# Projecting q and k by channels and placing them with on-chip DMAs, in a gated mix of segmented attention and a one-token FFN

## The chip, the cores and the metric

The kernel runs on one core of a Trainium2 chip. The metric is the device time of one execution in microseconds. The core has TensorE (PE; its weight loads are listed as PEld), VectorE (DVE), ScalarE (ACT) and GpSimd (POOL). SyncE (SP) computes nothing here; it issues all the DMAs, one after the other, in one queue.

## The reference

The input x has 2048 tokens of 640 channels. Branch A is attention with 32 heads of 20 channels over 4 segments of 512 tokens, each causal by itself, plus a memory that earlier segments have written. Branch B sends the one token with the highest router score through an FFN. A gate per token mixes the two.

```python
q, k, v = heads(x @ wq), heads(x @ wk), heads(x @ wv)
phi = lambda t: where(t > 0, t + 1, exp(t))
M = z = 0
for s in range(4):
    p = softmax(qs @ ks.T * scale + causal_mask)
    a_mem = phi(qs) @ M / (phi(qs) @ z + 1e-6)
    o = g * a_mem + (1 - g) * (p @ vs)        # g = sigmoid(beta), per head
    M, z = M + phi(ks).T @ vs, z + sum(phi(ks))
a = concat(o) @ wo
r = x @ w_r;  i = argmax(r)
b = x;  b[i] += sigmoid(r[i]) * (silu(x[i] @ w_gate) * (x[i] @ w_up)) @ w_down
out = sigmoid(x @ gate_w) * a + (1 - sigmoid(x @ gate_w)) * b
```

## The kernel before

**Units.** The heads are taken in four quarters (`hq`) of eight. A unit `u` is one quarter in one segment, 16 units in all. A group `n` is four heads of a unit, 32 groups in all.

**Projection (L249 to L284).** A chunk `q` is 128 tokens of a unit, 64 chunks. `load_x` brings the chunk of the transposed x, `split_x` makes a rounded high part (ScalarE) and a low part (GpSimd). 15 matmuls (5 slices of channels, 3 products of high and low parts) give `acc`, 128 tokens x 480 columns of q, k and v for eight heads. In the first quarter two more columns carry the router score and the gate. `evac` (L157) puts high, low and high again of q and k side by side in `qkn`, so that one matmul over 60 rows gives a logit of full accuracy, puts v into `va`, and phi of q and k into `phi`.

**Turning q and k (L179).** The logits need channels on the partitions. `stacks` transposes `qkn` on TensorE, four transposes for q and four for k in each chunk, and ScalarE copies the result into `qs` and `ks`, of which there are three each, one per unit.

**Memory (L189, L208, L220).** `memory_read` transposes phi of q, multiplies it with the memory `mbd`, and keeps the result in `nums`; `memory_norm` divides and gates. `memory_write` multiplies phi of k with v, one small matmul for each head and chunk, and adds into the diagonal blocks of `mbd`.

**Attention.** `a_step` computes logits for a pair of heads, queries on the partitions, and VectorE takes their maxima under the mask. `m_split` and `m_rows` (L310, L316) turn the negative maxima into two extra rows of `qs`: four transposes for each pair of heads, then a copy of two partitions by ScalarE and one by VectorE. `b_step` (L324) computes the logits again, keys on the partitions and the maxima already subtracted by those rows; ScalarE takes the exponential and GpSimd masks the diagonal. `pv_step` multiplies with v. `norm` (L368) transposes, divides, adds the memory part and, except in the last quarter, stores to `otok` in DRAM.

**Output.** `out_proj` transposes 128 rows of the attention's output, multiplies with wo in 30 matmuls of 320 columns, mixes in branch B and stores. The FFN's matmuls are spread over the middle of the run.

**Order.** TensorE's order is written out by hand: the loop at L622 goes through 34 groups of six slots. A slot has a `b_step` of group n and an `a_step` of the next group or the one after, and between them `fill` runs as much projection as the line `chunks[0] >= (at + 9) / 3 + 4.5` asks for, about 7.5 chunks ahead. The order on the other engines and on SP is made by a scheduler when the program is built; each executes it in order. PSUM has one buffer for `a`, one for `b`, one for `pv` and three of tag `misc` for everything else.

Of the kernel before, what the change touches and what calls it, by code (L numbers as in the profile page):

```python
# [7 lines left out]
F32 = mybir.dt.float32  # L8
# [10 lines left out]
KT = D // 128  # L19
NQ = 4  # L20
HQ = H // NQ
WQ = 3 * HQ * DH
FF = 1728
VW = DH + 1
ST = 2 + 3 * DH
SCALE = DH ** -0.5
NEG = -1e30

# [6 lines left out]
def tile_infini_mod(  # L35
# [51 lines left out]
    NB = 3  # L87
    qkn, qs, ks, va = [], [], [], []
    for i in range(2):
        t = one.tile([128, 2, HQ, 64], F32R, name=f"qkn{i}")  # L90
        nc.vector.memset(t[:, 0, :, :2].bitcast(F32), 0.0)
        nc.vector.memset(t[:, 1, :, :2].bitcast(F32), 1.0)
        nc.vector.memset(t[:, :, :, ST:].bitcast(F32), 0.0)
        qkn.append(t)
    for i in range(NB):
        qs.append(one.tile([128, HQ // 2, L], F32R, name=f"qs{i}"))
        ks.append(one.tile([128, HQ // 2, L], F32R, name=f"ks{i}"))
        t = one.tile([128, 4, HQ * VW + 11], F32, name=f"va{i}")
        nc.vector.memset(t, 1.0)
        va.append(t)  # L100
    phi = []
    for i in range(5):
        t = one.tile([128, 2, HQ, 32], F32, name=f"phi{i}")
        nc.gpsimd.memset(t, 0.0)
        phi.append(t)
    mneg = one.tile([128, 4, 2, 66], F32R, name="mneg")
    nc.gpsimd.memset(f32(mneg), 0.0)
    mbd = one.tile([128, 2, 128], F32, name="mbd")
    nc.gpsimd.memset(mbd, 0.0)
    rg = one.tile([128, 2, S // 128], F32, name="rg")  # L110

# [3 lines left out]


    W, wraw = {}, {}

    def load_w(key, k):
        if key[0] == "o":  # L120
            src = wo[128 * k:128 * k + 128, 320 * key[1]:320 * key[1] + 320]
        else:
            c0 = WQ * key[1] + (2 if key[1] else 0)
            src = wc[128 * k:128 * k + 128, c0:c0 + WQ + (0 if key[1] else 2)]
        t = pool.tile([128, WQ + 2], F32, tag="wraw", bufs=2, name="wraw")
        nc.sync.dma_start(t[:, :src.shape[1]], src)
        wraw[key, k] = t[:, :src.shape[1]]

    def split_w(key, k):
        raw = wraw.pop((key, k))  # L130
        n = raw.shape[1]
        hi = pool.tile([128, WQ + 2], F32R, tag="whi", bufs=2 * KT, name="whi")[:, :n]
        lo = pool.tile([128, WQ + 2], F32R, tag="wlo", bufs=2 * KT, name="wlo")[:, :n]
        split(hi, lo, raw, nc.vector)
        W[key, k] = hi, lo


    xraw, xhi, xlo = {}, {}, {}

    def load_x(q):  # L140
        t = pool.tile([128, KT, 128], F32, tag="xraw", bufs=2, name="xraw")
        s0 = (q % 16) * 128
        nc.sync.dma_start(t, xT[:, s0:s0 + 128].rearrange("(k p) t -> p k t", p=128))
        xraw[q] = t

    def split_x(q):
        xhi[q] = pool.tile([128, KT, 128], F32R, tag="xhi", bufs=2, name="xhi")
        xlo[q] = pool.tile([128, KT, 128], F32R, tag="xlo", bufs=2, name="xlo")
        split(xhi[q], xlo[q], xraw.pop(q), nc.gpsimd)
# [3 lines left out]
    done_units = [0]  # L153
    oldest = [0]
    chunks = [0.0]

    def evac(q, acc):  # L157
        u, c = divmod(q, 4)
        hq, s = divmod(u, SEG)
        t = qkn[q % 2]  # L160
        n = HQ * DH
        src = acc[:, :2 * n].rearrange("p (a h d) -> p a h d", a=2, d=DH)
        hi = sub(t, 2, [[HQ * 64, 2], [64, HQ], [1, DH]])
        nc.scalar.copy(hi, src)
        lo = sub(t, 2 + 2 * DH, [[HQ * 64 - DH, 2], [64, HQ], [1, DH]])
        nc.vector.tensor_tensor(out=lo, in0=src, in1=f32(hi), op=OP.subtract)
        hi2 = sub(t, 2 + DH, [[HQ * 64 + DH, 2], [64, HQ], [1, DH]])
        nc.vector.tensor_copy(hi2, f32(hi))
        v = sub(va[u % NB], c * (HQ * VW + 11), [[VW, HQ], [1, DH]])
        nc.scalar.copy(v, acc[:, 2 * n:3 * n].rearrange("p (h d) -> p h d", d=DH))  # L170
        a0, a1 = (0 if s > 0 else 1), (2 if s < SEG - 1 else 1)
        e = phi[q % 5][:, a0:a1, :, :DH]
        nc.scalar.activation(e, src[:, a0:a1], AF.Relu, scale=-1.0)
        nc.scalar.activation(e, e, AF.Exp, scale=-1.0)
        nc.vector.scalar_tensor_tensor(out=e, in0=src[:, a0:a1], scalar=1.0, in1=e, op0=OP.add, op1=OP.max)  # L175
        if hq == 0:
            nc.vector.tensor_copy(rg[:, :, 4 * s + c], acc[:, 3 * n:3 * n + 2])

    def stacks(q):  # L179
        u, c = divmod(q, 4)  # L180
        t = qkn[q % 2]
        for a, dst in ((0, qs), (1, ks)):
            tp = psum.tile([128, 4, 128], F32R, tag="misc", bufs=3, name="tp")
            for p in range(4):
                nc.tensor.transpose(tp[:, p, :], t[:, a, 2 * p:2 * p + 2, :].rearrange("p h r -> p (h r)"), identr)  # L185
            yield 4 * 56
            nc.scalar.copy(dst[u % NB][:, :, 128 * c:128 * c + 128], f32(tp))  # L187

    def memory_read(q):  # L189
        u, c = divmod(q, 4)  # L190
        tp = psum.tile([128, 2, 128], F32, tag="misc", bufs=3, name="tp")
        for g in range(2):
            nc.tensor.transpose(tp[:, g, :], phi[q % 5][:, 0, 4 * g:4 * g + 4, :].rearrange("p h r -> p (h r)"), identf)
        pt = pool.tile([128, 2, 128], F32, tag="pt", bufs=2, name="pt")
        nc.scalar.copy(pt, tp)
        yield 220
        nm = psum.tile([128, 2, 4, VW], F32, tag="misc", bufs=3, name="nm")
        for g in range(2):
            nc.tensor.matmul(nm[:, g], pt[:, g, :], mbd[:, g, :].rearrange("p (j r) -> p j r", r=32)[:, :, :VW],
                             start=True, stop=True)  # L200
        yield 430
        if c == 0:
            nums[u] = pool.tile([128, 4, HQ * VW], F32, tag="num", bufs=3, name="num")
        nc.scalar.copy(nums[u][:, c, :], nm.rearrange("p g j e -> p (g j e)"))
        if c == 3:
            memory_norm(u)

    def memory_norm(u):  # L208
        hq = u // SEG
        nu = nums.pop(u).rearrange("p c (h e) -> p c h e", e=VW)  # L210
        rm = pool.tile([128, 4, HQ], F32, tag="rm", bufs=2, name="rm")
        nc.vector.tensor_scalar(rm, nu[:, :, :, DH], 1e-6, None, op0=OP.add)
        nc.vector.reciprocal(rm, rm)
        gt = sub(gate, HQ * hq, [[0, 4], [1, HQ]])
        nc.vector.tensor_tensor(out=rm, in0=rm, in1=gt, op=OP.mult)
        rb = sub(rm, 0, [[HQ, 4], [1, HQ], [0, DH]])
        om[u] = nu[:, :, :, :DH]
        nc.gpsimd.tensor_tensor(out=om[u], in0=om[u], in1=rb, op=OP.mult)

    def memory_write(u):  # L220
        s = u % SEG
        mp = psum.tile([128, 2, 32], F32, tag="misc", bufs=3, name="mp")
        for g in range(2):
# [6 lines left out]
        for j in range(4):  # L230
            dst = mbd[32 * j:32 * j + 32, :, 32 * j:32 * j + VW]
            src = mp[32 * j:32 * j + 32, :, :VW]
            if s == 0:
                nc.vector.tensor_copy(dst, src)
            else:
                nc.vector.tensor_tensor(out=dst, in0=src, in1=dst, op=OP.add)

    def post(q):
        u, c = divmod(q, 4)
        s = u % SEG  # L240
        yield from stacks(q)
        if s > 0:
            yield from memory_read(q)
        if c == 3:
            if s < SEG - 1:
                yield from memory_write(u)
            done_units[0] = u + 1

    def projections():  # L249
        NCH = 4 * NQ * SEG  # L250
        for q in range(NCH):
            u, c = divmod(q, 4)
            hq, s = divmod(u, SEG)
            assert u < oldest[0] + NB
            if q + 2 < NCH:
                load_x(q + 2)
            if s == 2 and hq + 1 < NQ:
                key = ("q", hq + 1)
                if c == 0:
                    load_w(key, 0)  # L260
                load_w(key, c + 1)
                split_w(key, c)
# [451 lines left out]
```

## Time and profile before

| | |
|---|---|
| median of 3 runs | 866.21 us (865.5 to 866.72) |
| profiled execution, its own time | 871.42 us |
| span of the profiled execution | 869.7 us |
| mean granted TensorE clock | 0.929 |
| DVE busy | 539.0 us (62%) |
| ACT busy | 479.9 us (55%) |
| POOL busy | 236.0 us (27%) |
| DMA | 62.15 MB, 23.2% of 16 engines' time |

The span runs from the first to the last instruction. In a row of groups stand the source line, the engine, the operation, what it writes and reads, the shapes and the count; then busy time and mean duration, then the engine's idle time ahead of it with what ended that. In a timeline the columns are start, duration, engine, line and operation, and in brackets an idle time before it. The row of the granted clock gives it in tenths of full speed for 40 equal slices of the span. Rows of DMA issues give minimum, median and maximum of the time that the issuing instruction takes on SP, in ns.

### The profile page before, as it was taken

The page shows a single profiled execution, that of the slowest core. Times are in us where ns is not written, and L with a number is a line of the kernel's source. Part 1 is how long each engine was busy: PE and PEld are TensorE (multiplying, and loading weights), DVE is VectorE, ACT ScalarE, POOL GpSimd, SP SyncE. Part 2 cuts the span into 40 slices and gives each one's busy share as a digit, 9 for nine tenths or more (in the row PEclk, how much of TensorE's full clock was granted, in tenths as well). Part 3 has the DMA queues.
Part 4 walks back from the last instruction along what each step waited for, and adds up shares of the span by engine and source line. Part 5 has one row for each costly group of instructions (what it writes and reads, how often), then busy time and mean ns, then how long its engine had stood idle before and what let it go on. Part 6 is the DMA issues. An engine that isn't in the chain of part 4 may idle for free. (4 is left out here: it accounts for less than half of the span.)

```text
span 869.7 us, 15435 instructions
## 1 busy us (share of the span) xinstructions
PE 757.4 (87%) x5664; PEld 492.6 (57%) x5664; DVE 539.0 (62%) x1764; ACT 479.9 (55%) x915; POOL 236.0 (27%) x307
## 2 busy tenths in 40 slices
PE   5769898968898989989987979889998989999998
PEld 2646454634565555645554555545565545676787
DVE  5365665856666665767575665767666747575354
ACT  4536564735566655646564664656665747344422
POOL 3212322323333232233243232324232322111100
PEclk9989898979898998999998998989998989899999
DMA  6311011231101023524222232401010111133353
GB/s 183 116 30 32 16 44 34 77 58 26 52 26 52 16 61 98 176 82 136 81 57 76 72 102 67 137 23 52 27 48 29 32 32 39 47 105 107 122 164 124
DMA packets 68027, 62.15 MB, mean 71 GB/s; under 512 B 4262, under 2 KB 59312, under 8 KB 67952
## 3 DMA queue, kind: packets, MB, share of 16 engines
q1 hardware_dynamic: 67952, 61.17, 23.2%
q8 instruction: 45, 0.74, 0.4%
q14 instruction: 30, 0.25, 0.1%
HBM read 50.66 MB, written 9.19 MB: 69 GB/s over the span
## 5 line engine op out<-in xcount | busy, mean ns | idle before, releaser
L306 DVE CUSTOM_DVE_ANT_0 junk<-a,mask 128x512 bf16<-128x512 f32 (+3 forms) x512 | 248.8, 486 | 119.8 <-PE a L303 111.6
L336 ACT ACTIVATE p<-bt 128x768 f32<-128x768 f32 (+1 forms) x192 | 169.5, 883 | 162.2 <-PE bt L332 161.2
L339 POOL TENSOR_SCALAR_AFFINE_SELECT p<-p 128x256 f32<-128x256 f32 (+1 forms) x192 | 98.7, 514 | 391.9 <-ACT p L336 391.8
L274 PE MATMUL acc<-whi,xhi 128*128 128x480 f32 (+1 forms) x320 | 141.5, 442 | 7.7 <-ACT whi L113 7.5
L274 PE MATMUL acc<-wlo,xhi 128*128 128x480 f32 (+1 forms) x320 | 145.6, 455 | 1.3 <-DVE wlo L114 1.3
L274 PE MATMUL acc<-whi,xlo 128*128 128x480 f32 (+1 forms) x320 | 137.7, 430 | 0.0
L114 POOL TENSOR_TENSOR xlo<-xraw,xhi 128x640 fp32r<-128x640 f32 x64 | 99.3, 1551 | 121.4 <-ACT xhi L113 121.4
L303 PE MATMUL a<-ks,qs 62*128 62x256 f32 (+2 forms) x512 | 84.5, 367 | 41.7 <-DVE mx L306 41.7
L332 PE MATMUL bt<-qs,ks 62*128 62x256 f32 (+2 forms) x512 | 96.9, 417 | 13.4 <-ACT p L336 13.4
L352 PE MATMUL pv<-p,va 128*32 128x512 f32 (+3 forms) x1024 | 100.3, 515 | 0.0
L185 PE MATMUL tp<-identr,qkn 128*128 128x128 f32 x512 | 65.1, 252 | 35.1 <-DVE phi L175 12.1
L185 PEld LDWEIGHTS tp<-identr,qkn 128*128 128x128 f32 x512 | 54.7, 143 | 65.9 <-issue 35.2
L274 PEld LDWEIGHTS acc<-whi,xhi 128*128 128x128 f32 x320 | 63.4, 198 | 42.6 <-issue 24.3
L332 PEld LDWEIGHTS bt<-qs,ks 62*128 62x128 f32 x512 | 45.4, 195 | 66.7 <-issue 43.0
L303 PEld LDWEIGHTS a<-ks,qs 62*128 62x128 f32 x512 | 50.1, 203 | 54.9 <-DVE mx L306 38.7
L274 PEld LDWEIGHTS acc<-wlo,xhi 128*128 128x128 f32 x320 | 64.5, 201 | 29.2 <-issue 23.3
L322 DVE CAST qs<-mtp 2x512 fp32r<-2x512 f32 x64 | 44.1, 689 | 37.3 <-ACT qs L322 36.6
L274 PEld LDWEIGHTS acc<-whi,xlo 128*128 128x128 f32 x320 | 64.7, 202 | 3.2 <-issue 0.8
L113 ACT CAST xhi<-xraw 128x640 fp32r<-128x640 f32 x64 | 46.6, 729 | 23.5 <-PE acc L274 20.4
L322 ACT CAST qs<-mtp 2x512 fp32r<-2x512 f32 x64 | 36.8, 574 | 40.7 <-PE mtp L320 40.7
L187 ACT CAST qs<-tp 128x512 fp32r<-128x512 f32 x64 | 37.4, 584 | 38.2 <-PE tp L185 38.0
L352 PEld LDWEIGHTS pv<-p,va 128*32 128x32 f32 x1024 | 29.1, 119 | 51.3 <-issue 41.7
(102 smaller groups left out, 1083.8 us busy)
## 6 DMA issues: line engine op xcount, KB each, us to landing
xraw<-in_xT_dram SPq DMA_DIRECT2D x64, 320.0 KB
xf<-in_x_dram SPq DMA_DIRECT2D x16, 320.0 KB
out_dram<-xf SPq DMA_DIRECT2D x16, 320.0 KB
wt<-in_wg_dram SPq DMA_DIRECT2D x10, 432.0 KB
wt<-in_wu_dram SPq DMA_DIRECT2D x10, 432.0 KB
wt<-in_wd_dram SPq DMA_DIRECT2D x16, 270.0 KB
otok<-ou SPq DMA_DIRECT2D x12, 320.0 KB
ot<-otok SPq DMA_DIRECT2D x16, 240.0 KB
```

Source lines behind the costliest of these rows:

```text
L113: nc.scalar.copy(hi, raw)
L114: eng.tensor_tensor(out=lo, in0=raw, in1=f32(hi), op=OP.subtract)
L185: nc.tensor.transpose(tp[:, p, :], t[:, a, 2 * p:2 * p + 2, :].rearrange("p h r -> p (h r)"), identr)
L187: nc.scalar.copy(dst[u % NB][:, :, 128 * c:128 * c + 128], f32(tp))
L274: nc.tensor.matmul(acc[:, :width], a[:, k, :], b, start=i == 0, stop=i == 3 * KT - 1)
L303: nc.tensor.matmul(a[:, b, at:at + nw], q_, k_, start=True, stop=True)
L306: nc.vector.tensor_tensor_reduce(out=junk[:, :w], in0=a[:, b, at:at + w], in1=mask[:, L - w:], scale=1.0, scalar=-3e38, op0=OP.add, op1=OP ...
L322: copy(qs[u % NB][b:b + 2, 2 * g + p, :], f32(tp)[b:b + 2].rearrange("p a b -> p (a b)"))
L332: nc.tensor.matmul(bt[:, b, at:at + nw], k_, q_, start=True, stop=True)
L336: nc.scalar.activation(pt, bt[:, :, at:at + w], AF.Exp, scale=SCALE)
L339: nc.gpsimd.affine_select(out=d, in_=d, pattern=[[0, 2], [0, k], [1, 128]], base=0, channel_multiplier=-1, compare_op=OP.is_ge, fill=0.0)
L352: nc.tensor.matmul(pv[n][32 * j:32 * j + 32, L - w:], va[u % NB][:, c, VW * h:VW * h + 32], pt_tiles[n, j // 2, min(c, 2)][:, j % 2, at:at ...
```

## The change

Units become half the heads: 16 heads x 512 tokens, 8 units of four groups. Nothing changes in what is computed.

- q and k are projected with channels on the partitions. The weights are the stationary side, in five tiles T0 to T4 of 128 channels (`TILES`: 80 channels of a q group and pieces of k groups), and x streams by 512 tokens. v is still projected with tokens on the partitions, 320 columns for 16 heads (V0 to V3). Each of the nine jobs of a unit has 15 matmuls.
- `stacks` is gone. `evac_t` writes the high and the low part of a tile, and `place` copies each head's rows into `qs` and `ks` with three DMAs from SBUF to SBUF (high, high, low), each of up to 20 partitions x 512 values. A head that is split over two tiles takes two sets. `qs` and `ks` are now one buffer per group, five each.
- Because q is already transposed, `memory_read` needs no transposes. k has to be turned back for the memory: `keys` transposes each tile in fp32 (not in the last segment).
- `memory_write` multiplies four heads' phi of k (80 columns) with four heads' v (84 columns) at once and keeps the diagonal blocks with the mask `mask80`.
- `m_rows` turns all maxima of a group in one transpose; one copy takes them out of PSUM, and four DMAs put them into `qs` as rows 60 and 61 of each half.
- x is loaded and split in 8 x 5 pieces of 128 channels x 512 tokens. The weights of wc and wo, x, `ot`, `xf` and `y2` share four buffers of tag `raw`.
- `norm` stores every group to `otok`, the last ones too.
- `fill` runs the projection 3.4 groups ahead (`LEAD`), and one of its two calls in a slot moves behind `pv_phase`.

```diff
+TILES = (
+    ((0, 80, "q", 0, 0), (80, 128, "k", 0, 0)),
+    ((0, 80, "q", 1, 0), (80, 112, "k", 0, 48), (112, 128, "k", 1, 0)),
+    ((0, 64, "k", 1, 16), (64, 128, "k", 2, 0)),
+    ((0, 80, "q", 2, 0), (80, 96, "k", 2, 64), (96, 128, "k", 3, 0)),
+    ((0, 80, "q", 3, 0), (80, 128, "k", 3, 32)),
+)
+JOBS = ("T0", "T1", "V0", "V1", "T2", "V2", "V3", "T3", "T4")
+LAST = {"T1": 0, "T2": 1, "T3": 2, "T4": 3}
...
+    def load_x(u, k):
+        s = u % SEG
+        raw_tile(("x", u, k), xT[128 * k:128 * k + 128, L * s:L * s + L])
...
+    def place(kind, m, c0, hi, lo, r0, n):
+
+        assert m - NS < current[0]
+        dst = f32((qs if kind == "q" else ks)[m % NS])
+        base = {"q": (0, DH, 2 * DH), "k": (0, 2 * DH, DH)}[kind]
+        while n > 0:
+            h, d = divmod(c0, DH)
+            b, p = h % 2, h // 2
+            w = min(DH - d, n)
+            for src, at in ((hi, base[0]), (hi, base[1]), (lo, base[2])):
+                nc.sync.dma_start(dst[64 * b + at + d:64 * b + at + d + w, p, :], f32(src)[r0:r0 + w, :L])
+            c0, r0, n = c0 + w, r0 + w, n - w
+
+    def evac_t(u, j, acc):
+        s = u % SEG
+        hi = pool.tile([128, D], F32R, tag="hi", bufs=2, name="hi")
+        lo = pool.tile([128, D], F32R, tag="lo", bufs=2, name="lo")
+        nc.scalar.copy(hi[:, :L], acc)
+        nc.vector.tensor_tensor(out=lo[:, :L], in0=acc, in1=f32(hi)[:, :L], op=OP.subtract)
+        for r0, r1, kind, g, c0 in TILES[j]:
+            place(kind, 4 * u + g, c0, hi, lo, r0, r1 - r0)
...
+    def keys(u, j, e):
+        tp = psum.tile([128, 4, 128], F32, tag="misc", bufs=3, name="ktp")
+        for c in range(4):
+            nc.tensor.transpose(tp[:, c, :], e[:, 128 * c:128 * c + 128], identf)
+        for r0, r1, kind, g, c0 in TILES[j]:
+            if kind == "k":
+                nc.scalar.copy(kk[:, g, :, c0:c0 + r1 - r0], tp[:, :, r0:r1])
+        yield 4 * 60
+
+    def memory_read(u, g, e):
+        nm = psum.tile([128, 4, GW], F32, tag="misc", bufs=3, name="nm")
+        for c in range(4):
+            nc.tensor.matmul(nm[:, c, :], e[:GC, 128 * c:128 * c + 128], mbd[:, g, :], start=True, stop=True)
...
+        for g in range(4):
             for c in range(4):
-                for j in range(4):
-                    h = 4 * g + j
-                    nc.tensor.matmul(mp[32 * j:32 * j + 32, g, :VW], phi[(4 * u + c) % 5][:, 1, h, :],
-                                     va[u % NB][:, c, VW * h:VW * h + VW], start=c == 0, stop=c == 3)
-                yield 130
...
+                nc.tensor.matmul(mp[:, g, :], kk[:, g, c, :], va[u % 2][:, c, GW * g:GW * g + GW],
+                                 start=c == 0, stop=c == 3)
...
+                        if job[0] == "T":
+                            wh, wl = (t[:, 128 * k:128 * k + 128] for t in W["T", hf, j])
+                            a, b = ((wh, xh), (wl, xh), (wh, xl))[part]
+                            nc.tensor.matmul(acc, a, b, start=i == 0, stop=i == 3 * KT - 1)
...
+    def m_rows(n):
+        tp = psum.tile([128, 128], F32R, tag="misc", bufs=3, name="mtp")
+        nc.tensor.transpose(tp[:66, :], mneg[n % 2], identr)
+        mr = pool.tile([32, 128], F32, tag="mr", bufs=2, name="mr")
+        nc.scalar.copy(mr, f32(tp)[:32])
+        for b in range(2):
+            for r in range(2):
+                nc.sync.dma_start(f32(qs[n % NS])[64 * b + ST + r:64 * b + ST + r + 1].rearrange("r p (i t) -> r (p i) t", t=128),
+                                  mr[16 * b + 8 * r:16 * b + 8 * r + 8])
...
-        if hq < NQ - 1 and g == 1:
-            nc.sync.dma_start(otok[L * s:L * s + L, HQ * DH * hq:HQ * DH * hq + HQ * DH].rearrange(
-                "(c p) e -> p c e", p=128), ou.pop(u))
+        c0 = DH * (HH * hf + 4 * g)
+        nc.sync.dma_start(otok[L * s:L * s + L, c0:c0 + GC].rearrange("(c p) e -> p c e", p=128),
+                          ou.rearrange("p c j d -> p c (j d)"))
...
+    LEAD = 3.4
...
-        proj.until(lambda: chunks[0] >= (at + 9) / 3 + 4.5)
+        proj.until(lambda: chunks[0] >= at / 6 + LEAD)
```

In the built program SP has, for a unit in the middle, this order: T0's 21 placements, a store to `otok`, the four rows of one group's maxima; T1's 21, store, four rows; T2's 24, store, four rows; T3's 21, store; T4's 21, four rows; then the loads of x for a later unit. On TensorE the first `b_step` of a group stands about two slots behind that group's transpose of the maxima.

More of the change, by code (lines that the diff above doesn't have):

```diff
@@ L101, in tile_infini_mod @@
[L101 to L109, printed above, removed]
-    rg = one.tile([128, 2, S // 128], F32, name="rg")
+    mask80 = one.tile([GC, GW], F32, name="mask80")
+    nc.gpsimd.memset(mask80, 1.0)
+    for base, mult, step in ((0, 1, -DH), (DH - 1, -1, DH)):
+        nc.gpsimd.affine_select(out=mask80.rearrange("p (j e) -> p j e", e=VW), in_=mask80.rearrange("p (j e) -> p j e", e=VW),
+                                pattern=[[step, 4], [0, VW]], base=base, channel_multiplier=mult,
+                                compare_op=OP.is_ge, fill=0.0)
@@ new lines, in tile_infini_mod @@
+    NS = 5
+    qs, ks, va = [], [], []
+    for i in range(NS):
+        qs.append(one.tile([128, 2, L], F32R, name=f"qs{i}"))
+        t = one.tile([128, 2, L], F32R, name=f"ks{i}")
+        (nc.gpsimd if i % 2 else nc.vector).memset(f32(t), 1.0)
+        ks.append(t)
+    for i in range(2):
+        t = one.tile([128, 4, HH * VW + 11], F32, name=f"va{i}")
+        nc.gpsimd.memset(t, 1.0)
+        va.append(t)
+    kk = one.tile([128, 4, 4, GC], F32, name="kk")
+    mbd = one.tile([GC, 4, GW], F32, name="mbd")
@@ L151, in tile_infini_mod, with split_x @@
+    def split_x(u, k, eng=None):
+        hi = pool.tile([128, L], F32R, tag="xhi", bufs=KT + 2, name="xhi")
+        lo = pool.tile([128, L], F32R, tag="xlo", bufs=KT + 2, name="xlo")
+        split(hi, lo, raws.pop(("x", u, k)), eng or nc.gpsimd)
+        X[u, k] = hi, lo
     COST_MM = 1.0 / 2.4
     nums, om = {}, {}
-    done_units = [0]
-    oldest = [0]
+    groups = [0]
+    current = [0]
     chunks = [0.0]
[L157 to L212, printed above, removed]
-        nc.vector.reciprocal(rm, rm)
[L214 to L218, printed above, removed]
+    def rows(t, b0, b1):
+        return f32(t)[b0:b1]
@@ L230, in memory_write @@
[L230 to L247, printed above, removed]
@@ L657, in tile_infini_mod @@
             extra[:] = [f for f in extra if f.live]
[L658 to L663 removed]
+            if n == 28 and slot == 0:
                 for f in side:
```

356 lines of the change are left out of this document (204 added, 152 removed).

## The prediction

> **What bounds the kernel now.** I read the page's head first, then who waits for whom on TensorE, then a stretch of TensorE's timeline in the middle of the run, and last the DMA-issuing instructions of SP.
>
> ```profile
> span 869.7 us, 15435 instructions
> PE 757.4 (87%) x5664; PEld 492.6 (57%) x5664; DVE 539.0 (62%) x1764; ACT 479.9 (55%) x915; POOL 236.0 (27%) x307
> PEclk9989898979898998999998998989998989899999
> ```
> ```profile
> PE a L303 <- DVE mx L306: 41.7, 42, 3.5
> ```
> ```profile
> L185 PE MATMUL tp<-identr,qkn 128*128 128x128 f32 x512 | 65.1, 252 | 35.1 <-DVE phi L175 12.1 <-DVE qkn L168 11.2 <-DVE ou L382 4.2
> L374 PE MATMUL otp<-identf,pvs x128: 270/272/421, 106.3 to 830.8; 128*128 128x128 f32 x128
> ```
>
> TensorE is busy in every slice and idle for only 869.7 - 757.4 = 112.3 us. 41.7 of that is the maxima of the logits on VectorE, 35.1 is the wait ahead of the q/k transposes. So TensorE's issue order sets the time: work taken from it comes off, and any wait put into it goes on. The two `otp` ends give the pace: (830.8 - 106.3) / 31 = 23.4 us for a group of four heads.
>
> Prices on TensorE are start-to-start distances in one timeline, not busy times, since matmuls overlap:
>
> ```profile
> 611.83 0.51 PE L332 MATMUL bt<-qs,ks 62*128 62x256 f32 x4 [0.67 <-ACT p L336]
> 613.11 0.44 PE L303 MATMUL a<-ks,qs 62*128 62x384 f32 x2 [0.77 <-DVE mx L306]
> ...
> 615.88 3.13 PE L352 MATMUL pv<-p,va 128*32 128x512 f32 x16
> 618.94 0.71 PE L274 MATMUL acc<-whi,xhi 128*128 128x480 f32 x1
> ...
> 628.02 0.60 PE L374 MATMUL otp<-identf,pvs 128*128 128x128 f32 x4
> 628.55 0.45 PE L332 MATMUL bt<-qs,ks 62*128 62x384 f32 x2
> ...
> 636.57 1.71 PE L352 MATMUL pv<-p,va 128*32 128x512 f32 x16
> 638.21 0.48 PE L274 MATMUL acc<-whi,xhi 128*128 128x480 f32 x1
> 638.53 0.38 PE L274 MATMUL acc<-wlo,xhi 128*128 128x480 f32 x1
> 638.85 0.51 PE L332 MATMUL bt<-qs,ks 62*128 62x512 f32 x2
> ...
> 639.62 0.54 PE L185 MATMUL tp<-identr,qkn 128*128 128x128 f32 x4
> 639.99 0.46 PE L274 MATMUL acc<-whi,xlo 128*128 128x480 f32 x1
> 640.29 0.38 PE L274 MATMUL acc<-whi,xhi 128*128 128x480 f32 x1
> 640.51 0.46 PE L185 MATMUL tp<-identr,qkn 128*128 128x128 f32 x4
> ...
> 642.76 0.57 PE L199 MATMUL nm<-mbd,pt 128*128 128x84 f32 x4
> 643.12 0.46 PE L274 MATMUL acc<-whi,xlo 128*128 128x480 f32 x1
> 643.42 0.38 PE L274 MATMUL acc<-whi,xhi 128*128 128x480 f32 x1
> 643.64 0.40 PE L320 MATMUL mtp<-identr,mneg 128*66 128x128 f32 x4
> 643.97 0.86 PE L352 MATMUL pv<-p,va 128*32 128x256 f32 x16
> ```
>
> From it: a projection matmul of 480 columns 0.22, four stack transposes 0.37, four fp32 transposes 0.53, four maxima transposes 0.33, four `nm` 0.36, and 0.08 more on the matmul after each change of kind (0.30 against 0.22).
>
> **TensorE's side: what goes and what comes.**
> - Gone: 128 batches of stack transposes, 128 x (0.37 + 0.08) = 58 us. The maxima's transposes shrink from 64 batches of four to 32 single ones: 64 x 0.41 - 32 x 0.18 = 20. Of `memory_read` 48 transpose batches go, about 48 x 0.22 = 11.
> - New: `keys` transposes 5 tiles in each of 6 units, 30 x (0.53 + 0.08) = 18. The memory write becomes 192 instructions of the `nm` kind, 48 x (0.36 + 0.08) - about 10 now = 11.
> - Moved: 600 matmuls of 512 columns (0.22 x 512/480 = 0.235) and 480 of 320 stand in for 960 of 480. The row below gives 4.66/30 = 0.155 for 320 columns, so 141 + 74 - 211 = 4 more.
>
> ```profile
> 854.61 4.66 PE acc L550 x30
> ```
>
> Net work: -58 - 20 - 11 + 18 + 11 + 4 = -56 us. The 35.1 us ahead of `tp` lose their waiter. Bounds are 0 (VectorE's lateness reappears at `a`) and 35; I take 30. VectorE loses the 48.4 us copy and the 44.1 us cast below, ScalarE 36.8 and the two evictions of L187; neither bounds, so I credit only 9 of the 41.7 us ahead of `a` (bounds 0 and 20). Without anything on DMA's side the span would be 869.7 - 56 - 30 - 9 = 775, a group 20.4 us.
>
> ```profile
> L168 DVE CAST qkn<-qkn 128x320 fp32r<-128x320 f32 x64 | 48.4, 756 | 0.3
> L322 DVE CAST qs<-mtp 2x512 fp32r<-2x512 f32 x64 | 44.1, 689 | 37.3 <-ACT qs L322 36.6
> L322 ACT CAST qs<-mtp 2x512 fp32r<-2x512 f32 x64 | 36.8, 574 | 40.7 <-PE mtp L320 40.7
> ```
>
> **SP's side.** What the transposes did is now done by `place`: a unit of 16 heads x 512 tokens issues 108 DMAs (21, 21, 24, 21 and 21 after tiles T0 to T4), `m_rows` 4 a group, `norm` one. That is about 139 a unit with the loads, over 1,200 in all, every one on SP. Their price:
>
> ```profile
> L364 SPq DMA_DIRECT2D ot<-otok x16: 319/320/339, 702.3 to 849.4; - x16
> L365 SPq DMA_DIRECT2D ot<-ou x16: 470/471/982, 702.7 to 849.8; - x16
> L388 SPq DMA_DIRECT2D otok<-ou x12: 366/377/388, 128.4 to 651.0; - x12
> L403 SPq DMA_DIRECT2D sel<-top x2: 230/230/231, 187.0 to 202.9; - x2
> L493 SPq DMA_DIRECT2D yrow<-y x1: 545/545/545, 549.1 to 549.1; - x1
> ```
> ```profile
> 783.12 0.42 SPq L559 DMA_DIRECT2D out_dram<-xf  x1
> 783.60 0.47 SPq L365 DMA_DIRECT2D ot<-ou  x1
> ```
> ```profile
> 184.01 0.30 SPq L397 DMA_DIRECT2D row<-rrow  x1
> ...
> 186.72 0.27 DVE L399 TENSOR_REDUCE top<-row 1x1 f32<-1x128 f32 x1 [3.91 <-DMA row<-rrow]
> ```
>
> No row shows 20 partitions of 2 KB from SBUF to SBUF. The nearest is `ot<-ou`, the only SBUF-to-SBUF one: 0.47. A one-element store takes 0.23, the four-row `yrow` 0.545. I take 0.43, just under `ot<-ou`, plus the gap of 0.06 (783.12 + 0.42 to 783.60): 0.48; bounds 0.28 and 0.65. From issue to use I take 2.4 us (184.31 to 186.72). A unit then holds SP for 108 x 0.48 + 16 x 0.48 + 15 x 0.42 = 66 us of 4 x 20.4 = 82: no overload, but an in-order queue four fifths full, with bursts of 10 to 12 us.
>
> **Where TensorE meets it.** Two instructions now wait for SP: the first `bt` of a group for its maxima's rows, the first `a` for its placed q and k. Everything on TensorE stands behind them, and `a` and `bt` feed VectorE and ScalarE. I set the built program's order of a late unit against the prices above; a group there sums to 17.3 us without waits (projection 6.8, six `b`/`a` pairs of 0.6 to 0.77 make 4.0, `pv` 1.64 + 0.8, transposes 1.4, memory 1.3, changes of kind 1.4), so each distance is lengthened by 20.4/17.3 = 1.18. ScalarE's and VectorE's evictions of a tile take 2.0 us, from these rows and a little queueing:
>
> ```profile
> L528 DVE TENSOR_TENSOR ol<-ttp,oh 128x512 fp32r<-128x512 f32 x16 | 11.1, 692 | 12.8 <-ACT oh L527 12.7
> L527 ACT CAST oh<-ttp 128x512 fp32r<-128x512 f32 x16 | 9.3, 584 | 21.9 <-PE ttp L526 21.7
> ```
>
> 1. After T4. In SP's order the rows of the next group stand behind T4's 21 DMAs. They land 2.0 + 21 x 0.48 + 4 x 0.48 + 2.4 = 16.4 us after T4's last matmul. TensorE reaches `bt` after nine projection matmuls, two `b`/`a` pairs, half a `pv`, a `keys` batch and the maxima's transpose, 7.3 x 1.18 = 8.6. Stall 7.8.
> 2. After T0, rows behind its burst and an `otok` store: 2.0 + 10.1 + 0.4 + 1.9 + 2.4 = 16.8 against 13.8 x 1.18 = 16.3 (all of T1, most of a v tile, four pairs, half a `pv`). Stall 0.5.
> 3. After T3, the third group's first `a` needs 15 of the burst: 2.0 + 7.2 + 2.4 = 11.6 against 7.1 x 1.18 = 8.4 (ten projection matmuls, two and a half pairs, three transpose batches, the other half of `pv`). Stall 3.2.
> 4. After T1 and T2: 5.3 us from the maxima's transpose to landed rows, against 5.0 x 1.18 = 5.9. Nothing; at the upper price 2 to 7.
>
> 11.5 us a unit, 92 over 8. At 0.28 only the first stays, 2.8 us, 24 in all; at 0.65 the sum is 12 + 5 + 6 + 2 = 25 a unit, 200 in all.
>
> A wait also slows what follows: after gaps of 0.67 and 0.77 the sixteen `pv` starting at 615.88 take 3.06 us against 1.64 at 636.57, and the matmuls near them likewise, some 2.7 us in all. One such loss for each long stall, 8 x 2.7 = 22; bounds 0, if the clock would have been down there anyway, and 45. The Trainium skill (TensorE: Matmul & The Clock Gate, HAM oscillation) has the half clock come after idle gaps over about 3.4 us and last about as long; by that each stall would cost an estimated 1.7 us and the term be 14. The trace disagrees on the threshold, since gaps under 0.8 us preceded the slow stretch.
>
> Start: the first `a` waits for 42 placements, so it begins no earlier than now, with two chunks' projection less done: 30 x 0.22 = 7 us (bounds 0 and 15).
>
> Sum: 775 + 92 + 22 + 7 = 896 of span. The median of the runs, 866.21, lies 3.5 under the profiled span, so 893. Hidden at no cost: x loaded 40 times instead of 64, fewer x splits (POOL was 27% busy), and `otok` stored for every group, read only at the end.
>
> **Rivals.**
> - *Issues are cheap* (35%). The rows land before TensorE comes. For it: one-row issues of 0.23 to 0.30, and VectorE's relief, of which I credit 9 us. Against it: `ot<-ou` at 0.47, sixteen times alike. At 0.33 with the gap, stall 1 is 2 + 25 x 0.33 + 2.4 - 8.6 = 4.0, stall 3 1.0: 775 + 40 + 10 + 4 = 829, so 825; at 0.28 about 803. It decides on the near side of about 0.42 an issue. The Trainium skill (DMA: Bandwidth & Descriptors, Issuing engines are not separate DMA queues) calls the sequencer's time for a DMA usually small beside the transfer, which is this rival's world; the 0.47 row against 40 KB says otherwise.
> - *SP becomes the bound* (17%). At 0.65 (the four-row 0.545 and a gap and second wait) a unit's SP work is 124 x 0.65 + 6 = 87 us, over the 82 of TensorE, and every burst runs into the next: 775 + 200 + 30 + 9 = 1014.
> - *Nothing gained or lost* (3%): gain and stalls cancel.
>
> **Numbers.** The forecast of late rows has 45%, with its own range 850 to 950. A measurement here tells 0.2% (1.7 us) from nothing. Faster 35%, same 3%, slower 62%. The range 795 to 1005 takes in the cheap issue at its lower end and most of the SP-bound case.
>
> **What would show it.** Right: `tp` and L168 gone; SP's placements at 0.4 to 0.5 us; the first `bt` after T4 ended by a DMA into `qs`, 6 to 10 us, once a unit; `a` of the third group ended by placements; the granted clock down behind them. Wrong: placements under 0.38 us and TensorE's waits still mostly `mx`; or SP issuing without a pause.

## The result, and the profile after

| | before | changed |
|---|---|---|
| median | 865.86 us (865.07 to 866.72, 4 runs) | 1086.18 us (1081.12 to 1087.16, 4 runs) |
| span of the profiled execution | 869.7 us | 1083.9 us |
| mean granted TensorE clock | 0.929 | 0.811 |

The ratio is 1.2533, with a 95% interval of 1.2491 to 1.2574: the changed kernel takes a quarter longer. Slower was the forecast's direction, but its 893 us, and its range up to 1005, missed the size.

The head of the page of the changed kernel, its row of the granted clock, and the two rows that share out the chain that ended last:

```profile
span 1083.9 us, 14132 instructions
PE 748.8 (69%) x4496; PEld 496.2 (46%) x4496; DVE 447.2 (41%) x1507; ACT 357.4 (33%) x594; POOL 192.1 (18%) x299
PEclk8587589869995978768876969877788788868999
...
SPq 39%; PE 33%; DMA 10%; DVE 7%; issue 5%; ACT 4%; POOL 1%; DVEq 0%; ACTq 0%; POOLq 0%
SPq L212 31%; PE acc L328 7%; PE acc L614 5%; PE acc L333 5%; SPq L393 5%; PE bt L403 5%; DMA qs<-mr 4%; PE a L372 3%; DVE junk L375 3%; PE pv L423 3%; ACT p L407 2%; DMA raw<-in_xT_dram 1%; PE mp L262 1%; PE ktp L236 1%; SPq L143 1%
```

VectorE, ScalarE and GpSimd all do less than before, and no engine that computes is busy for more than 69% of the span. TensorE was idle for 112.3 us before and is for 1083.9 - 748.8 = 335.1 now. The largest part of the last chain is `SPq L212`, the issuing of the placements.

Who waits for whom on TensorE (total us, times, longest us):

```profile
PE bt L403 <- DMA qs<-mr: 179.7, 48, 21.6
PE ktp L236 <- DVE phi L227: 38.6, 26, 4.2
PE a L372 <- DMA ks<-lo: 24.8, 4, 12.8
PE ffn L553 <- DMA wt<-in_wd_dram: 17.2, 2, 13.8
...
PE ffn L527 <- DMA wt<-in_wg_dram: 12.8, 1, 12.8
```

Before, the longest sums were 41.7 us for the maxima and 35.1 us ahead of the q/k transposes, which no longer exist; now it is 179.7 us for the maxima's rows. The DMAs that bring these rows stand in SP's queue, and these are SP's instructions at the placements' line and at the rows' line (ns minimum/median/maximum, first and last start in us):

```profile
L212 SPq DMA_DIRECT2D ks<-hi x320: 554/707/1748, 33.3 to 957.2; - x160
L212 SPq DMA_DIRECT2D qs<-hi x256: 706/708/1319, 24.1 to 950.6; - x128
L212 SPq DMA_DIRECT2D ks<-lo x160: 530/706/1444, 34.8 to 958.0; - x160
L212 SPq DMA_DIRECT2D qs<-lo x128: 706/707/1218, 25.8 to 951.3; - x128
...
```
```profile
L393 SPq DMA_DIRECT2D qs<-mr x128: 623/635/717, 84.5 to 995.0; - x128
```

864 placements at 0.707 hold SP for 611 us. The first and the last of the `hi` ones are 957.2 - 24.1 apart, which is 116.6 us for each of the eight units; the prediction had 81.6 for TensorE without stalls. A part of SP's timeline after a tile T4, and TensorE in the same stretch (start, duration; in brackets the idle time ahead and what ended it):

```profile
709.73 1.50 SPq L212 DMA_DIRECT2D ks<-hi  x2
711.28 0.71 SPq L212 DMA_DIRECT2D ks<-lo  x1
712.03 1.46 SPq L212 DMA_DIRECT2D ks<-hi  x2
713.53 0.71 SPq L212 DMA_DIRECT2D ks<-lo  x1
714.34 2.71 SPq L393 DMA_DIRECT2D qs<-mr  x4
717.15 0.86 SPq L510 DMA_DIRECT2D wt<-in_wu_dram  x2
```
```profile
704.38 0.39 PE L328 MATMUL acc<-xlo,whi 128*128 128x512 f32 x1
716.97 0.76 PE L403 MATMUL bt<-qs,ks 62*128 62x512 f32 x1 [12.20 <-DMA qs<-mr]
...
721.10 0.78 PE L328 MATMUL acc<-xhi,wlo 128*128 128x512 f32 x1
721.67 0.57 PE L328 MATMUL acc<-xlo,whi 128*128 128x512 f32 x1
722.07 0.39 PE L328 MATMUL acc<-xhi,whi 128*128 128x512 f32 x1
```

SP issues without a pause here: three placements take 712.03 - 709.73 = 2.30 us, 0.77 each with the gaps, and the four rows follow at 0.68. While TensorE stands still for 12.20 us, SP does nothing but this. Then TensorE is slow: `bt` takes 0.76, where the same shape takes 0.46 behind short waits (285.83 and 307.76 in the rows further below), and `acc` still takes 0.78 at 721.10, against 0.39 at 722.07.

### The profile page after: what moved, and what is told of

It reads as the page before. It is cut to its first block, busy times and chain, and to the rows that moved or that the text cites. A ratio compares the mean times of both kernels' runs of the same rounds, so it can differ in the third digit from the quotient of the medians.

```text
span 1083.9 us, 14132 instructions
## 1 busy us (share of the span) xinstructions
PE 748.8 (69%) x4496; PEld 496.2 (46%) x4496; DVE 447.2 (41%) x1507; ACT 357.4 (33%) x594; POOL 192.1 (18%) x299
## 4 chain that ended last, share of the span: by engine, by line
SPq 39%; PE 33%; DMA 10%; DVE 7%; issue 5%; ACT 4%; POOL 1%; DVEq 0%; ACTq 0%; POOLq 0%
SPq L212 31%; PE acc L328 7%; PE acc L614 5%; PE acc L333 5%; SPq L393 5%; PE bt L403 5%; DMA qs<-mr 4%; PE a L372 3%; DVE junk L375 3%; PE pv L423 3%; ACT p L407 2%; DMA raw<-in_xT_dram 1%; PE mp L262 1%; PE ktp L236 1%; SPq L143 1%
## 5 line engine op out<-in xcount | busy, mean ns | idle before, releaser
L403 PE MATMUL bt<-qs,ks 62*128 62x256 f32 (+2 forms) x512 | 123.5, 454 | 191.2 <-DMA qs<-mr 179.7
L372 PE MATMUL a<-ks,qs 60*128 60x256 f32 (+2 forms) x512 | 100.0, 394 | 38.2 <-DMA ks<-lo 24.8
L328 PE MATMUL acc<-xhi,whi 128*128 128x512 f32 x200 | 94.0, 470 | 8.2 <-ACT xhi L150 8.2
L328 PE MATMUL acc<-xhi,wlo 128*128 128x512 f32 x200 | 96.7, 484 | 0.0
L328 PE MATMUL acc<-xlo,whi 128*128 128x512 f32 x200 | 94.3, 472 | 0.9 <-POOL xlo L151 0.9
L372 PEld LDWEIGHTS a<-ks,qs 60*128 60x128 f32 x512 | 58.9, 221 | 48.8 <-DVE mx L375 18.8
L333 PE MATMUL acc<-wlo,xhi 128*128 128x322 f32 (+1 forms) x160 | 60.3, 377 | 0.0
L333 PE MATMUL acc<-whi,xhi 128*128 128x322 f32 (+1 forms) x160 | 60.2, 376 | 0.0
L328 PEld LDWEIGHTS acc<-xhi,whi 128*128 128x128 f32 x200 | 44.1, 221 | 27.6 <-issue 12.9
L333 PE MATMUL acc<-whi,xlo 128*128 128x322 f32 (+1 forms) x160 | 56.0, 350 | 0.0
L614 PE MATMUL acc<-whi,oh 128*128 128x320 f32 x160 | 52.8, 330 | 2.6 <-DVE xf L621 1.5
L614 PE MATMUL acc<-whi,ol 128*128 128x320 f32 x160 | 51.6, 322 | 0.2 <-DVE ol L592 0.2
L236 PE MATMUL ktp<-identf,phi 128*128 128x128 f32 x120 | 23.5, 328 | 38.6 <-DVE phi L227 38.6
```

What stands on the lines that cost most here:

```text
L328: nc.tensor.matmul(acc, a, b, start=i == 0, stop=i == 3 * KT - 1)
L333: nc.tensor.matmul(acc[:, :w], a, b, start=i == 0, stop=i == 3 * KT - 1)
L372: nc.tensor.matmul(a[:, b, at:at + nw], q_, k_, start=True, stop=True)
L403: nc.tensor.matmul(bt[:, b, at:at + nw], k_, q_, start=True, stop=True)
L614: nc.tensor.matmul(acc[:, :n], a_[:, 128 * k:128 * k + 128], b_[:, n * b:n * b + n], start=i == 0, stop=i == 3 * KT - 1)
```

## The experiments

The theory (A in the expectations): the number of DMAs that SP issues, at 0.7 us each whatever they carry, sets the pace. The chief rivals: the transfers' bytes or their landing (C), or only the order, the rows standing behind a burst (D). F and H are about the `keys` batch, whose 38.6 us in the table of waits are a second loss; other letters are rivals of single runs. Each time is beside the median of the kernel before on the same chip. Most variants were executed once, and then no interval is given.

**One high copy less.** 36 placements a unit, 288 in all, are left out.

```diff
-            for src, at in ((hi, base[0]), (hi, base[1]), (lo, base[2])):
+            for src, at in ((hi, base[0]), (lo, base[2])):
```


> Leaves out the second copy of the high part: each head gets two placements instead of three (288 DMAs of 864 fewer; the rows keep a constant). Theory A (SP's issue time of 0.71 us and a gap of 0.05 for each placement is the bound): 288 x 0.75 = 216 us of SP's queue go, so the time falls from 1086 to 870 to 920, not all of the 216 because TensorE's own limit of some 775 to 800 us and the remaining bursts come near. Theory B (the latency of a placement, from issue to landing, is what TensorE waits for, whatever the count): under 60 us gained, above 1020.

892.65 us (before 863.69). The waits of TensorE in this kernel:

```profile
PE bt L405 <- DMA qs<-mr: 53.2, 23, 10.5
PE ktp L238 <- DVE phi L229: 46.1, 29, 4.3
```

1086.18 - 892.65 = 193.5 us for 288 DMAs, 0.67 each, nearly the whole 0.75 that one holds SP. The wait for the rows falls by 126.5, and the clock rises to 0.883. The `keys` wait stays.

**Half the columns.** As many DMAs, each with half the bytes; the other half of q and k is not placed.

```diff
-... at + d + w, p, :], f32(src)[r0:r0 + w, :L])
+... at + d + w, p, :L // 2], f32(src)[r0:r0 + w, :L // 2])
```


> The same number of placements, each of 256 columns instead of 512: half of q and k is left out of the placement, and half of the bytes. Theory A (issue time on SP): a placement still takes about 0.70 us on SP, and the time stays at 1060 to 1090. Theory C (the DMA engines' transfer of 40 KB is what holds SP back): a placement falls to about 0.4 us and the time to 900 to 960.

1062.42 us. The price did not move with the bytes:

```profile
L214 SPq DMA_DIRECT2D qs<-hi x256: 706/708/1417, 27.5 to 927.7; - x128
```

So a placement costs its issue, not its 40 KB. The 24 us gained lie in SP's pauses: the stretch from the first to the last placement is 26 us shorter (908 us against 935), while SP issues in it for as long as before (738 us against 741).

**The maxima's rows from ScalarE.** This takes `m_rows`' DMAs out of SP's order, with all placements left on SP.

```diff
-                nc.sync.dma_start(f32(qs[n % NS])[64 * b + ST + r: ...
+                nc.scalar.dma_start(f32(qs[n % NS])[64 * b + ST + r: ...
```


> Only the four row DMAs of m_rows go to ScalarE's queue, placements stay on SP. Theory D (only the order hurts: rows stuck behind bursts, 180 us of TensorE's waits): these waits shrink to under 60 us and the time falls to 880 to 930. Theory A (SP's total): SP is rid of 128 x 0.68 = 87 us, the wait moves from the first bt of a group to the first a, which waits for placements; 980 to 1030.

987.21 us. The wait of `bt` for the rows is out of TensorE's ten longest, and 99 us are gained, but the kernel stays 123 us slower than before. The rows cost ScalarE 0.63 each, and its exponentials now wait behind them (ScalarE's issues, then a row of its waits, then TensorE's):

```profile
L393 ACTq DMA_DIRECT2D qs<-mr x128: 627/628/1224, 79.1 to 891.4; - x128
```
```profile
ACT p L407 <- DMA qs<-mr: 48.6, 17, 3.2
```
```profile
PE ktp L236 <- DVE phi L227: 59.7, 28, 4.2
PE a L372 <- DMA ks<-lo: 37.1, 9, 14.3
```

With the rows out of the way, the next customers of SP are late: the placed q and k (37.1 us against 24.8), and the FFN's weights (54.1 us against 33.3). The time came out where A had it and not D, so order alone is not the cause; but the work that ScalarE's issues hold up is a part of the 123 us that this run does not separate.

**Three queues.** Each of the three copies from its own engine.

```diff
-            for src, at in ((hi, base[0]), (hi, base[1]), (lo, base[2])):
-                nc.sync.dma_start(...
+            for src, at, eng in ((hi, base[0], nc.sync), (hi, base[1], nc.scalar), (lo, base[2], nc.gpsimd)):
+                eng.dma_start(...
```


> The three copies of a head go to three queues: high on SP, second high on ScalarE's, low on GpSimd's. Theory A: SP keeps 288 x 0.75 + 128 x 0.68 + some 100 = 400 us, ScalarE gets 288 x 0.75 = 216 on top of 357 busy, GpSimd about 288 x 1 on top of 192; no queue is the bound any more, the waits for DMA fall under 60 us and the time to 790 to 850, under the 866 of before. If the placements' landing or the DMA engines were the limit: above 1000.

1058.17 us, a plain miss. SP is relieved (`bt` waits 4.3 us for the rows), but the time is lost elsewhere. TensorE's longest wait, and a stretch of ScalarE:

```profile
PE ktp L236 <- DVE phi L227: 196.8, 29, 8.2
```
```profile
517.99 0.59 ACT L219 CAST hi<-acc 128x512 fp32r<-128x512 f32 x1 [1.88 <-PE acc L328]
518.60 6.40 ACTq L212 DMA_DIRECT2D ks<-hi  x8
525.05 0.60 ACT L225 ACTIVATE phi<-acc 128x512 f32<-128x512 f32 x1 [6.48 <-DMA ks<-hi]
```

ScalarE evicts `hi`, issues eight placements for 6.40 us and only then starts phi. The `keys` batch stands in TensorE's order for the phi, and everything behind it. The wait has moved from the queue of SP to the engine that computes.

**Two copies from GpSimd.** The same edit with SP, GpSimd, GpSimd.

```diff
+            for src, at, eng in ((hi, base[0], nc.sync), (hi, base[1], nc.gpsimd), (lo, base[2], nc.gpsimd)):
```


> First high copies stay on SP, second high and low copies go to GpSimd's queue, none to ScalarE's. Theory A with what the three-queue run showed (0.50 us an issue on GpSimd, none of its issues waited for by TensorE; the loss there came from phi behind ScalarE's issues): SP 288 x 0.75 + 128 x 0.68 + 95 = 400 us, GpSimd 576 x 0.5 + 192 = 480; no queue is the bound, 820 to 880, the wait of ktp for phi back under 60 us. Rival E (any compute engine's queue that issues a burst holds up its own work): GpSimd's masks of p come up to 7 us late, 40 bursts, TensorE waits for p ahead of pv; 950 to 1050.

838.41 us (before 873.72), 248 under the changed kernel. In this run TensorE waits 0.9 us in all for GpSimd's work, and GpSimd issues the same copy in 0.505 us:

```profile
L212 POOL DMA_DIRECT2D ks<-lo x160: 505/509/527, 20.8 to 714.9; - x160
```
```profile
PE ktp L236 <- DVE phi L227: 43.6, 29, 4.1
```

The `keys` wait is now the largest: the batch stands in TensorE's order before its phi can be ready. Two ways to put it later were tried.

**The same, memory work late in the group.** The slots that draw from the memory work are 10, 12, 13, 14.

```diff
-                        if i in (4, 7, 10, 13):
+                        if i in (10, 12, 13, 14):
```


> The two-queue version (first high copies on SP, the other two on GpSimd), and the transposes of keys and the memory read and write start behind the tenth matmul of the next job instead of the fourth. Theory F (with SP no longer the bound, the next wait is ktp for phi, 43.6 us in the run before, and TensorE's order sets the time again): this wait falls under 20 us, the time from 838 to 800 to 820. Rival G (those waits are cover for others; TensorE stands at the next wait instead): 830 to 845.

826.4 us (816.28 to 828.88, 6 runs), ratio 0.9512 (0.9441 to 0.9583), a little above what was expected. The `keys` wait falls to 2.2 us, but `bt` waits 31.0 for the rows, against 12.3.

**The same, memory work one job later.** `keys`, `memory_read` and `memory_write` go to a list `fresh`, which joins the work list at the end of the next job.

```diff
-                tail.append(keys(u, j, e))
+                fresh.append(keys(u, j, e))
...
+                tail.extend(fresh)
+                fresh.clear()
```


> As the run before it, but the memory work of a tile is put off by a whole job (some 8 us) and spread as in the changed kernel. Theory F: the wait of ktp and nm for phi goes to nearly 0, 785 to 815, the fastest of all. Rival G: 830 to 845.

792.82 us (786.0 to 797.7, 4 runs), ratio 0.9097 (0.8997 to 0.9196): faster than both kernels. The head of its page, TensorE's longest waits, and SP's placements:

```profile
PE 695.9 (87%) x4496; PEld 468.4 (59%) x4496; DVE 446.0 (56%) x1507; ACT 354.6 (45%) x594; POOL 474.5 (60%) x875
```
```profile
PE pv L426 <- POOL p L413: 14.0, 13, 2.9
PE a L375 <- DVE mx L378: 13.2, 16, 2.3
PE bt L406 <- DMA qs<-mr: 12.7, 11, 5.1
```
```profile
L212 SPq DMA_DIRECT2D ks<-hi x160: 554/707/1177, 29.1 to 678.8; - x160
L212 SPq DMA_DIRECT2D qs<-hi x128: 706/717/1424, 25.8 to 676.6; - x128
...
DMA to landing us min/median/max: 1.7/2.4/6.4
```

A unit takes (678.8 - 25.8) / 8 = 81.6 us, the four groups of 20.4 that the prediction gave TensorE without DMA cost. So the projection by channels gains once most placements are off SP: 4% with the queues alone (one execution), 9% with the memory work put off as well.

**The changed kernel, memory work late in the group.** The edit of the slots alone, all DMAs on SP.

> The changed kernel with only the later memory work; all placements on SP. Theory A (SP's issue is the bound): the 38.6 us that TensorE waits ahead of ktp are cover for SP, the time stays at 1070 to 1095. Rival H (TensorE's waits add up): 1040 to 1055.

1101.97 us, no gain (16 us above the changed kernel, in one execution, and 7 above the range that A gave). `bt` waits 222.2 us for the rows against 179.7, and the `keys` wait is gone: while SP is the bound, another wait taken away only lengthens the one for SP.

**Through DRAM.** 18 stores a unit put the tiles into scratch in DRAM, and 48 loads of 20 x 2 x 512 values bring two heads at a time back, all on SP: 66 DMAs instead of 108, and no copy from SBUF to SBUF.

```diff
+        for part, src in (("hi", hi), ("lo", lo)):
+            nc.sync.dma_start(scr[kind, part, u % 2][c:c + n, :], f32(src)[r0:r0 + n, :L])
...
+            for b in range(2):
+                nc.sync.dma_start(dst[64 * b + DH * i:64 * b + DH * i + DH], v[b])
```


> High and low parts go to DRAM (18 stores a unit) and come back two heads at a time (48 loads of 20 partitions x 2 x 512), 66 issues a unit instead of 108 and twice the traffic. Theory A (issue time on SP): with stores at some 0.4 us, loads at 0.45 to 0.7 and a wait of some 2.5 us for the stores of each tile SP needs 45 to 58 us a unit, under TensorE's 82; the time falls to 820 to 880. Theory B (landing time): every placement lands some 3 us later than in the changed kernel and the traffic doubles, so no gain or slower, 1060 or more.

868.79 us (before 873.72), with twice the way for the data:

```profile
L222 SPq DMA_DIRECT2D qs<-sqhi x128: 273/334/767, 27.2 to 742.2; - x128
```
```profile
PE bt L420 <- DMA qs<-mr: 22.0, 15, 5.6
```

A load with twice the placement's bytes costs SP 0.33 us, less than half of its price, and the rows come late by 22.0 us instead of 179.7. That SP's time and not the distance decides is shown here from the other side.

**Through DRAM, memory work one job later.** Both edits together.

> High and low parts through DRAM, all 66 issues a unit on SP (0.30 to 0.42 us each in the earlier run), and the memory work put off by a whole job. Theory A with F (the price and number of SP's issues, then phi): SP needs 18 x 0.42 + 48 x 0.36 + 11 + 7 = 43 us a unit, so nothing stands before TensorE but itself; 868 less the 63 us that ktp and nm waited for phi, 800 to 825. Rival B (landing through DRAM is too late): the wait moves to bt and a, 850 to 870.

846.02 us (844.92 to 847.13, 2 runs), ratio 0.9756 (0.9598 to 0.9914). A gain is clear of noise, but one of less than 2% lies within the interval, and the time is 21 us above the range that A and F together gave. Part of it is that the way through DRAM lands late: `a` waits 21.8 us for `sqlo`, against 6.7 without the later memory work, and `bt` 28.8 for the rows, against 22.0.

**All three copies from GpSimd, memory work one job later.**

```diff
+            for src, at, eng in ((hi, base[0], nc.gpsimd), (hi, base[1], nc.gpsimd), (lo, base[2], nc.gpsimd)):
```


> All three copies on GpSimd's queue, rows and loads on SP, memory work put off by a whole job. Theory A (a queue under its limit costs nothing): GpSimd has 864 x 0.55 + 192 = 670 us of some 800, SP is free for the rows; but its bursts are 11 us, so its masks of p and its low parts of x come late: 800 to 840, slower than the 793 of the shared version. Rival E (bursts on a compute engine's queue do not matter as long as its total fits): 780 to 795.

904.99 us (903.23 to 906.75), ratio 1.0436 (1.0263 to 1.0609), more than expected. Now GpSimd is the queue, and its own masks stand in it:

```profile
PE pv L426 <- POOL p L413: 95.1, 32, 8.7
```

864 issues of 0.505 us are 436 us beside 192 of its work. GpSimd is busy for 616.9 us of a span of 901.5, so the total fits; the bursts alone make the masks late, which is against this run's E. The split of one third and two thirds was better than either end.

**The price of an issue by itself.** Copies of 512 fp32 values per partition were added to the end of the kernel before, four of each kind. Its time, 910.54 us, says nothing here.

> The kernel before, with copies of 4 to 128 partitions x 512 behind its end that nobody reads: SBUF to SBUF from SP and from GpSimd, and of 20 partitions between SBUF and DRAM. Its time is not of interest. If the number of partitions sets the issue time on SP, 128 partitions take more than 20 (0.71) and 4 less; if two SBUF ends set it, 20 partitions take about 0.33 from or to DRAM and 0.7 within SBUF; on GpSimd 0.50 throughout. If 20 partitions are dear because few engines share them, 16, 32 and 128 are cheaper than 20.

Rows of 20 partitions from SP and GpSimd, and of 128 from SP (ns minimum/median/maximum):

```profile
L684 SPq DMA_DIRECT2D pse<-psrc x4: 707/722/763, 874.3 to 877.6; - x4
L684 POOL DMA_DIRECT2D pge<-psrc x4: 505/514/526, 875.3 to 878.3; - x4
...
L684 SPq DMA_DIRECT2D psh<-psrc x4: 465/470/478, 888.0 to 892.9; - x4
```

All medians of SP, from SBUF to SBUF unless noted, us:

| 4 | 8 | 12 | 16 | 20 | 32 | 64 | 128 | 20, half the columns | 20, from DRAM | 20, to DRAM |
|---|---|---|---|---|---|---|---|---|---|---|
| 0.617 | 0.624 | 0.725 | 0.528 | 0.722 | 0.528 | 0.478 | 0.470 | 0.742 | 0.296 | 0.355 |

Rows of 128 partitions were the only ones of their way, SBUF to SBUF, that the trace of before showed.

## Why the prediction was wrong, step by step

- *What goes from the engines*: right. TensorE's net 56 us off 757.4 give 701; where no queue slows the clock it is 695.9 (one job later, two copies from GpSimd). VectorE lost 539.0 - 447.2 = 91.8 us against the two rows of 48.4 and 44.1. The 30 us credited for the wait ahead of the transposes came back in the changed kernel as the wait of `keys`, 38.6; put a job later, it is gone. The span without DMA cost was given as 775, and that kernel has 795.5, with waits of 12.7 us for the rows, 11.7 for the first placed k and 14.0 for masks still in it.
- *The price of a placement on SP*: the step that failed. It was taken as 0.48 with the gap, from the `ot<-ou` row, with bounds of 0.28 and 0.65. It is 0.707, and 0.75 to 0.77 with the gap: outside the bounds. The nearest row was nearest in kind but not in partitions: within SBUF, the 20 partitions of a head, not the 40 KB, make the price. That the choice went below this row, 0.43 against 0.47, had no reason either. (Two slips change little: 0.43 with the gap of 0.06 is 0.49, and eight times 2.8 is 22, not 24.) The rows of the maxima were taken as 0.48 too and are 0.68. So a unit's SP work is 108 x 0.755 + 16 x 0.68 + 15 x 0.42 (the prediction's others, taken over) = 99 us, against TensorE's 82. To that come SP's own waits: the twelve largest between the first and the last placement, with 33.4 us for `hi` ahead, add up to 122 us, 15 a unit. Together 114; the measured unit is 116.6.
- *The verdict on the queue*: "no overload, but an in-order queue four fifths full" is false; it is overfull. That was the rival in which SP becomes the bound, and its mechanism came true, past its price of 0.65 and so past its 1014.
- *Stall 1, after T4*: right in place, too small. Seven such waits of 12.2 to 21.6 us make 106.5 of the 179.7; the prediction had 8 x 7.8. With 0.755 and 0.68 its formula gives 2.0 + 21 x 0.755 + 4 x 0.68 + 2.4 - 8.6 = 14.4, but that this meets the measured waits is partly luck, since other terms are off both ways. For the wait at 716.97 shown above:

```profile
691.33 0.39 PE L328 MATMUL acc<-xlo,whi 128*128 128x512 f32 x1
```
```profile
696.20 0.71 SPq L212 DMA_DIRECT2D ks<-lo  x1
...
698.52 1.53 SPq L212 DMA_DIRECT2D qs<-hi  x2
```

  T4's last matmul ends at 691.72 and its first placement starts at 698.52, 6.8 us later instead of 2.0, because SP issues T3's burst until 696.91 and three other DMAs behind it: one burst runs into the next. From the first row's issue (714.34) to `bt` it is 2.6 us instead of 4 x 0.68 + 2.4 = 5.1, as the first `bt` starts before the fourth row's issue ends. And TensorE comes to `bt` at 704.77, 13.0 us behind T4 instead of 8.6. So 6.8 + 15.8 + 2.6 - 13.0 = 12.2.

  One unit's longer waits of `bt` for the rows, from T4 to the next T4:

```profile
238.09 0.76 PE L403 MATMUL bt<-qs,ks 62*128 62x512 f32 x1 [14.57 <-DMA qs<-mr]
...
266.85 0.47 PE L403 MATMUL bt<-qs,ks 62*128 62x512 f32 x1 [2.83 <-DMA qs<-mr]
...
285.83 0.46 PE L403 MATMUL bt<-qs,ks 62*128 62x512 f32 x1 [1.39 <-DMA qs<-mr]
...
307.76 0.46 PE L403 MATMUL bt<-qs,ks 62*128 62x512 f32 x1 [3.76 <-DMA qs<-mr]
...
348.25 0.76 PE L403 MATMUL bt<-qs,ks 62*128 62x512 f32 x1 [13.56 <-DMA qs<-mr]
```

  The landing itself did not fail: 2.4 us were taken, counted from the end of an issue, and in the kernel with two copies from GpSimd and the memory work one job later the median is 2.4 from an issue's start, over both issuers.
- *Stalls 2 to 4*: 2 and 4 were put at 0.5 and nothing; the three short waits above are 2.83 behind T0's burst (266.85), and 1.39 and 3.76 behind T1's and T2's. Stall 3, the third group's first `a` at 3.2, did not come: the 24.8 us of `a` for `ks<-lo` are four waits, all in the first 56 us. They belong to the start, which was put at 7. TensorE's waits for the rows and for `a` together are 204.5 us; the prediction had 92, and 200 at the price of 0.65.
- *The clock*: right in kind, too small. Behind the stall at 716.97 matmuls are slow until about 721.7, 4.7 us. The same 4496 matmuls are busy for 748.8 - 695.9 = 53 us more; 22 was taken, with 45 as the bound. The Trainium skill (TensorE: Matmul & The Clock Gate, The HAM clock gate) has the clock halved after an idle window of about 3.4 us, and back after about 3.4 us of steady work; the slow stretch here is of that order, a little longer. The prediction's 14 us by that rule counted eight stalls. TensorE has 23 gaps of over 3.4 us here and 5 in the kernel with 695.9; by that rule the 18 more, at the prediction's 1.7 us each, make an estimated 31, still short of 53.
- *Two waits that the prediction did not have*: the `keys` batch stands in TensorE's order ahead of its phi, 38.6 us, and the late loads of the FFN's weights behind SP's bursts, over 30 us. The prediction named the DMAs that bring rows and q and k, but not the loads that stand in the same queue.
- *What would show it wrong*: "SP issuing without a pause" was given as the sign. It is what the timeline shows in the stretch above; over the whole it is interrupted by the 122 us of SP's own waits.

With the measured terms the prediction's sum is 775 + 204.5 + 53 + 38.6 + 30 = 1101 against the span of 1083.9. Of the 188 us by which the span exceeded the predicted one of 896, the longer waits for rows and for placed q and k are some 105 (204.5 against 92 and the start's 7), the clock behind them 31; the two waits left out, 68.6, are more than the 51 that remain, as the sum is 17 us above the span.

Not settled: why SP paused less with half the columns, and why the late memory work of the changed kernel lost 16 us (one execution each).

## What to carry to other kernels

Before data movement goes from an engine to DMAs, multiply the number of DMAs by the issue time of exactly that kind of copy (both ends, partition count) and hold the product against the bound engine's time; a row of another shape is no price, and the bytes may not matter at all. When a queue in order is overfull, the wait shows up at its most urgent customer, and reordering hands it to the next one: fewer DMAs or another issuing engine is what helps. That the total fits is not enough: what stands behind a burst comes late all the same, as GpSimd's masks showed. The engine that takes them over must not have, behind its bursts, something that the bound engine waits for: two of the three copies given to GpSimd gained 248 us here, one to GpSimd and one to ScalarE only 28 (one execution each).

## What the runs showed of the hardware

- From SBUF to SBUF, SP's issue time went with the partitions and not with the bytes: 0.47 to 0.53 us for 16, 32, 64 and 128, 0.62 for 4 and 8, and 0.72 for 12 and 20, also with half the columns. From DRAM into SBUF 20 partitions took 0.296, and the other way 0.355. The Trainium skill (DMA: Bandwidth & Descriptors, Why a DMA increments its semaphore by 16 and not by 1) has a copy from SP run on the largest number of engines up to 16 that divides its partitions, the issuer itself writing the rest of the 16. The split between 16 engines and fewer fits the first eight columns of the table, but the load of 20 partitions from DRAM at 0.296 shows that it isn't this alone. The cause is open.
- GpSimd issued the 20-row copy in 0.505 us in the kernels (0.514 by itself), and 0.49 to 0.55 from 4 to 128 partitions, while ScalarE took 0.728 for it, like SP. For this copy GpSimd was the cheapest issuer.
- The same page (Issuing engines are not separate DMA queues) calls the sequencer's time for a DMA usually small beside the transfer, and lets several issuers save only that time. Here that time is 0.707 us beside about 2.4 from issue to landing, and taking two thirds of these issues off SP was worth 248 us.
